# T5-bias attention with a bilinear FFN: a new order for the opening's loads and steps

## The chip, the cores and the metric

The kernel runs on one core of a Trainium2 chip. The metric is the device time of one execution in microseconds; smaller is better. Engines: PE (TensorE, matmuls and transposes), DVE (VectorE), ACT (ScalarE), POOL (GpSimd) and SP (SyncE, which here only issues DMAs).

## The reference

Eight batches of eight heads, 576 positions, head size 64. Each head's scores get a bias that depends on the distance of the two positions alone (32 buckets), then softmax and the product with the values. The result, 4608 tokens of 512 features, goes through a bilinear FFN without a nonlinearity.

```python
scores = scale * np.matmul(q, k.transpose(0, 1, 3, 2))      # q, k, v: 8 x 8 x 576 x 64
bias = bias_table[bucket]                                   # bucket from |i - j|, 32 x 8 table
scores = scores + bias.transpose(2, 0, 1)[None, :, :, :]
attn = softmax(scores)
x = (attn @ v), heads side by side                          # 4608 x 512
a = x @ w_a                                                 # 512 x 1536
b = x @ w_b
out = (a * b) @ w_out                                       # 1536 x 512
```

## The kernel before

**Tiling.** A *pair* is two neighbouring heads of one batch; pairs are numbered 0 to 31, four to a batch. The 576 positions are 512 main ones (four tiles of 128) and a tail of 64. Scores are kept with the keys on the partitions, so exponentials come out of ACT as the left operand of the product with the values, which carries a column of ones for the softmax's sum. The bias is applied after the exponential: it is multiplied by exp(bias), taken from *band* tiles `W` (one for each head pair; `Wt` for the tail) that DVE reads backwards. A band depends on the distance alone: the 32 x 8 table is read, its last row is subtracted, ACT takes the exponential, PE spreads it over 256 distances with a one-hot matrix, DVE copies that into a row of ones, SP stores it to DRAM (`bias_tab`), and DMAs read it back with one step of offset for each partition. A filler is a matmul on a tile of zeros (`warm_up`).

**The opening and the steady part.** Pairs 0 to 7 (batches 0 and 1) and the first FFN layer on batch 0's 512 main tokens are done by an opening that is written out by hand as a list of tokens, `opening`, which `step` turns into instructions one by one. Each engine takes its own instructions in the list's order. Pairs 8 to 31 follow in a steady part (`steady`, `slot_step`) that weaves their attention with the FFN of earlier batches. In the opening q and k are transposed on PE; from batch 2 on by DMA.

**Tokens** (the first digit is the pair p, or the FFN's block of 128 hidden features):

- `<name` issues a load: q, k (`k23` is pairs 2 and 3; `q123h0` is the first 256 positions of q of pairs 1 to 3), v0, v1 (batch 0's values, heads 0 to 3 and 4 to 7), t and u (tails of q and k of batches 0 and 1), vt (tails of v), W and R (upper and lower columns of a band), Wt, wa, wb, wo (FFN weights, in thirds). All go to POOL's queue except `W0`, on SP. They are all issued ahead of the opening's other tokens in program order.
- `YQ0`, `YK0`: pair 0's q and k, loaded as fp32 on SP by `load_first`, are converted to bf16. `TQ`, `TK`, `TZ`: PE transposes of q, k and tails (`TQ00` is the first half of the queries of pair 0; `TQ0` does both); `CQ`, `CK`, `CZ`: their copies out of PSUM.
- `Sphu`: score matmuls of pair p, query half h, key tiles 2u and 2u+1 (pairs 4 to 7: `Spt`, one key tile). `E` their exponential on ACT, `M` the multiplication by the band on DVE. `KS`, `EK`: the tail keys of all four pairs of batch 0. `T`, `ET`, `MT`: a pair's tail.
- `AVph`: product with the values; `N`: normalisation; `X`, `CX`: PE transpose and copy to `xn`, the FFN's input. `V`: copy of the values next to their ones.
- `FA`, `FB`, `HA`, `G`: one block of x @ w_a and x @ w_b on PE, the first's copy on ACT, their product on DVE (a, b: first and second 256 tokens; f: all 512).
- `PV`, `PC`, `PU`, `PX`, `PF`: zeroing of padding. `w2`: two fillers. `LH`, `LV`, `TH`: loads and DMA transposes for batch 2.
- `:A` is ACT, `:D` DVE.

The scores of the first four pairs share two PSUM buffers with tails, so a score half waits until the exponential before the last has read its buffer. What the change touches:

```python
    nc.sync.dma_start(out=cn_sb[:, :], in_=cn_handle.ap())            # one-hot matrix and identity
    load_first(q, kq32[1])                                            # L228
    load_first(k, kq32[0])
    nc.scalar.dma_start(out=bt_sb[0:NB, :], in_=bias_table)           # L234; bl_sb (the last row): L235
    warm_up(5)
    ...
    pad_z(0, 0)                                                       # zeroes half of ZB[0], L193
    pad_z(0, 1)
    nc.vector.tensor_copy(out=tab_sb[0:H, c0:c0 + NR], in_=tps[0:H, 0:NR])   # L260; the store to bias_tab: L268
```

Lines of the profile that the text uses: L129 and L153 loads of q, k, v; L263 bands; L281 FFN weights; L329 DVE copies; L474 scores (`qkh`), L480 their exponential (`ath`); L696 FFN matmuls (`pa`, `pb`).

Of the kernel before, what the change touches and what calls it, by code (L numbers as in the profile page):

```python
# [13 lines left out]
def kernel(  # L14
# [11 lines left out]
    nc = tc.nc  # L26
# [5 lines left out]
    B, H, S, Dh = 8, 8, 576, 64  # L32
    NB = 32
# [27 lines left out]
    NR = 256  # L61
# [127 lines left out]
    def load_w_out():  # L189
        nc.gpsimd.dma_start(out=wo_sb[:, :, :], in_=moe_w_out.rearrange("(t p) n -> p t n", p=128))  # L190

    def pad_z(b, hh):
        nc.vector.memset(ZB[b][64 * hh:64 * hh + 64, :, :, Dh - Dh * hh:128 - Dh * hh], 0.0)  # L193
# [3 lines left out]
        nc.vector.memset(tl[i][64:128, :, :, 0:Dh], 0.0)  # L197

    def pad(eng, x, p0, p1):
        if eng is nc.vector:  # L200
            nc.vector.memset(x, 0.0)
            return
        n = int(np.prod(x.shape[1:]))
        z = (zero_sb.bitcast(FP32) if x.dtype == FP32 else zero_sb)[p0:p1, 0:n]
        if len(x.shape) == 3:
            z = z.rearrange("p (a b) -> p a b", b=x.shape[2])
        elif len(x.shape) == 4:
            z = z.rearrange("p (a b c) -> p a b c", b=x.shape[2], c=x.shape[3])
        nc.scalar.activation(out=x, in_=z, func=ACTF.Copy)
# [17 lines left out]
    def load_first(x, dst):  # L227
        nc.sync.dma_start(out=dst.rearrange("p (h x) -> p h x", x=256),  # L228
                          in_=x[0, 0:2, 0:SM, :].rearrange("h (p t) d -> p h (t d)", t=NM))

    nc.sync.dma_start(out=cn_sb[:, :], in_=cn_handle.ap())
    load_first(q, kq32[1])
    load_first(k, kq32[0])
    nc.scalar.dma_start(out=bt_sb[0:NB, :], in_=bias_table)  # L234
    nc.scalar.dma_start(out=bl_sb[0:NB, :],  # L235
                        in_=bass.AP(tensor=bias_table.tensor, offset=(NB - 1) * H,
                                    ap=[[0, NB], [1, H]]))
    nc.vector.memset(zero_sb[:, :], 0.0)
    nc.vector.memset(tab_sb.bitcast(FP32)[0:H, :], TWO_ONES)
    pad_ones(0)  # L240
# [5 lines left out]
    def warm_up(n, dst=None):  # L246
        for _ in range(n):
            nc.tensor.matmul(out=(warm if dst is None else dst)[:, :], lhsT=zero_sb[:, 0:128],
                             rhs=zero_sb[:, :], start=True, stop=True)

    warm_up(5)
    nc.scalar.activation(out=eb_sb[0:NB, :], in_=bt_sb[0:NB, :], func=ACTF.Exp)
    tps = ps_ff.tile([128, 512], FP32, tag="ffn", name="tab_ps")
    nc.tensor.matmul(out=tps[0:H, 0:NR], lhsT=eb_sb[0:NB, :], rhs=oh_sb[0:NB, :],
                     start=True, stop=True)
    warm_up(2)
    c0 = S - 1 - NR // 2
    pad_z(0, 0)
    pad_z(0, 1)
    nc.vector.tensor_copy(out=tab_sb[0:H, c0:c0 + NR], in_=tps[0:H, 0:NR])  # L260

    def load_w(hp, y0, y1, eng):
# [22 lines left out]
    def load(name):  # L285
        if name[0] in "qk" and name[1:2].isdigit():
            ps, _, half = name[1:].partition("h")
            p0, n = int(ps[0]), len(ps)
            if half:
                load_qh(2 * p0, 2 * p0 + 2 * n, int(half))  # L290
            else:
                b, h = divmod(2 * p0, H)
                (load_q if name[0] == "q" else load_k)(b, h, h + 2 * n)
        elif name[0] in "tu":
            load_compact(int(name[0] == "u"), int(name[1] == "k"))
        elif name in ("v0", "v1"):
            load_v(0, 4 * int(name[1]), 4 * int(name[1]) + 4)
        elif name[:3] == "vb1":
            load_v(1, *((0, 4) if name[3] == "a" else (4, 8)))
        elif name[:2] == "vt":  # L300
            load_vt_part(int(name[2] == "1"), "ab".index(name[-1]))
        elif name == "wo":
            load_w_out()
        elif name[:2] == "Wt":
            load_wt("ab".index(name[2]))
        elif name[0] in "WR":
            load_w(int(name[1]), *((320, NY) if name[0] == "W" else (0, 320)), nc.sync if name in ('W0',) else nc.gpsimd)
        else:
            load_weights(*((moe_w_a, wa_sb) if name[1] == "a" else (moe_w_b, wb_sb)), int(name[2]))

# [478 lines left out]
    def v_next(s):  # L789
# [7 lines left out]
    ACT = nc.scalar  # L797

    opening = """
        <q123h0 <k1 <tk <vtb <k23 <W1 <W0 <v0 <vta <tq <W2 <W3 <v1 <Wta <q123h1 <R0 <Wtb <R1 <k4 <wa0  # L800
        <wb0 <R2 <uq <q5 <q4 <R3 <k5 <wa1 <q7 <wb1 <k6 <uk <k7 <vb1a <vb1b <vt1a <q6 <wb2 <vt1b <wa2 <wo
        PC0:A PX0:D YQ0:A PC1:A PU0:D PV0:A PX1:D TQ0 YK0:D TK0 CQ00:A CQ01:D CK0:D TQ10 PF1:A CQ10:D
        S000 E000 PV1:D S001 E001 TK1 CK1:D TQ30 TZ1 CZ1:D S011 CQ30:D E011 S101 TQ20 CQ20:D E101 M101
        S100 E100 TK3 CK3:D KS EK M000 TK2 S301 E301 CK2:D w2 S200 E200 M100 M001 w1 S201 E201 V0:D
        PU1:D w2 S300 E300 M200 M201 AV00 TZ0 AV10 S010 CZ0:A N00 T0 N10 E010 X10 X00 CX00:A V1:D AV20
        CX10:A TQ11 TQ21 M301 M300 ET0 AV30 CQ11:A S110 CQ21:A N20 M010 M011 PW:A MT0 S111 TQ31 E110 X20
        CQ31:A E111 T1 ET1 N30 M110 X30 CX20:D CX30:D AV01 T2 TK4 M111 S210 ET2 E210 FA0a HA0a N01 T3
        MT1 X01 AV11 CK4:D CX01:A PF0:D LH ET3 N11 S211 E211 FB0a FA1a HA1a X11 G0a MT2 CX11:D S310 E310
        FB1a G1a S311 M210 FA2a FB2a HA2a E311 TQ5 TQ4 CQ4:A M211 FA3a AV21 CQ5:A S42 G2a S43 FB3a TZ0x
        MT3 M311 HA3a M310 TK5 E42 N21 FA4a HA4a CZ0x:D AV31 LV CK5:D X21 E43 TQ7 CQ7:A G3a N31 S41 E41  # L810
        S52 E52 FB4a FA5a HA5a CX21:D G4a M43 TK6 X31 CX31:D FB5a S40 E40 CK6:D S53 G5a FA0b HA0b TZ1x
        M41 CZ1x:D FB0b G0b S51 E53 FA1b HA1b TK7 FB1b FA2b E51 M52 HA2b CK7:D S50 G1b V2:D FB2b FA3b
        E50 V3:D G2b HA3b T4 M40 FB3b G3b S70 M42 ET4 MT4 FA4b FB4b T5 HA4b M53 E70 G4b TQ6 ET5 M51
        CQ6:A AV40 N40 FA5b S71 E71 S73 MT5 M50 FB5b HA5b AV41 S72 E73 G5b N41 M71 FA6f M73 T6 E72 M72
        ET6 MT6 AV50 FB6f HA6f N50 S62 S61 E62 G6f M62 FA7f HA7f AV51 N51 TH S60 E61 M61 FB7f G7f E60
        M60 S63 E63 FA8f HA8f T7 ET7 M63 M70 FB8f G8f AV60 FA9f FB9f N60 MT7 AV70 HA9f G9f FA10f HA10f
        FB10f N70 AV71 G10f FA11f HA11f FB11f N71 X71 AV61 X70 G11f N61 CX71:D CX70:D
    """

    h0 = (0, 1)  # L820
# [2 lines left out]
    def step(token):  # L823
# [6 lines left out]
            load(token[1:])  # L830
            return
        name, _, e = token.partition(":")
        eng = ACT if e == "A" else nc.vector
        kind = name.rstrip("0123456789abfx")
        num = name[len(kind):]
        if kind in ("FA", "HA", "FB", "G"):
# [21 lines left out]
        if kind == "TQ":  # L858
            tr_qh(p, i[1]) if len(i) > 1 else tr_q(p)
        elif kind == "CQ":  # L860
            copy_qh(p, i[1], eng) if len(i) > 1 else copy_q(p, eng)
        elif kind == "TK":
            tr_k(p)
        elif kind == "CK":
            copy_k(p, eng)
        elif kind == "TZ":
            tr_tails(second, p)
        elif kind == "CZ":
            copy_tails(second, p, eng)
        elif kind == "KS":  # L870
            tail_keys0()
        elif kind == "EK":
            ex_keys0()
        elif kind == "S":
            qk_half(p, i[1], (i[2],)) if first else qk(p, 0, (i[1],))
        elif kind == "E":
            ex_half(p, i[1], i[2]) if first else ex(p, i[1])
        elif kind == "M":
            mul_half(p, i[1], i[2]) if first else mul(p, i[1])
        elif kind == "T":  # L880
            qk_tail(p)
        elif kind == "ET":
            ex_tail(p)
        elif kind == "MT":
            mul_tail(p)
        elif kind == "V":
            b, g = divmod(p, 2)
            v_in(b, 4 * g, 4 * g + 4, eng)
        elif kind == "AV":
            av_mm(p, jqs, *((ps_ff, "ffn") if first and i[1] == 0 and p % 2 else ()))  # L890
        elif kind == "N":
            av_norm(p, jqs)
            if 4 <= p < 7 and i[1] == 1:
                t_x(p)
        elif kind == "X":
            tr_x(p, jqs)
        elif kind == "CX":
            copy_x(p, jqs, eng)
        elif kind == "YK":
            copy(eng, kn[0][:, 0:512], kq32[0])  # L900
        elif kind == "YQ":
            copy(eng, qn[0][:, 0:512], kq32[1])
        elif kind == "PV":
            pad_vt(0, p, eng)
        elif kind == "PC":
            pad_vt(1, p, eng)
        elif kind == "PU":
            pad_blocks(ZB[1], p, eng)
        elif kind == "PF":
            pad_blocks(tl[0], p, eng)  # L910
        elif kind == "PX":
            pad_x(p, eng)
        elif kind == "PW":
            copy(eng, Wt_sb[:, :, 0:64], Wt_sb[:, :, 64:128])
        elif kind == "LH":
            load_k(2, 0, 4)
            load_q(2, 0, 4)
            load_tails(2)
            load_v(2, 0, 4)
        elif kind == "TH":  # L920
            t_half(2, 0)
        elif kind == "LV":
            load_vt(2)
        else:
            raise ValueError(token)
# [187 lines left out]
```

## Time and profile before

| | us |
|---|---|
| median of 3 runs | 400.9 (400.34 to 401.28) |
| profiled execution, device time | 401.12 |
| its span in the profile | 399.3 |
| PE busy, idle | 390.6, 8.7 |
| DVE, ACT, POOL busy | 240.9, 255.9, 133.4 |

The span is what the trace covers; 1.8 us of the device time lie around it. A row of the timeline has the start in us, the busy time, the engine, the line, the operation with its output and inputs, the count, and in brackets the idle time of the engine before it and what ended that. Durations overlap when instructions of one engine follow each other, so a step counts by the distance of the starts where the rows show it. Times in the text are us from the span's start.

### The profile page before, as it was taken

Reading aid. Unit: us, or ns where it says so; the run is one execution under the profiler, and the core shown is the slowest. Engines: PE = TensorE matmul, PEld = TensorE weight load, DVE = VectorE, ACT = ScalarE, POOL = GpSimd, SP = SyncE. Lnnn points to the kernel's source line nnn. Section 1 sums busy time; section 2 is a strip of 40 time slices with the busy share of each in tenths; the row PEclk is TensorE's granted clock in tenths of the full one; section 3 lists DMA queues with packets and bytes.
Section 4 is the critical chain, followed back from the end, with each engine's and each line's share of the span. In section 5 each row is a group of like instructions: output and inputs, shape, how many; then the busy total and the mean of one; then the engine's idle time right before and its main releaser. Section 6 shows DMA issues by size and latency. Waiting matters only on the chain.

```text
span 399.3 us, 13162 instructions
## 1 busy us (share of the span) xinstructions
PE 390.6 (98%) x5614; PEld 231.2 (58%) x5626; DVE 240.9 (60%) x565; ACT 255.9 (64%) x386; POOL 133.4 (33%) x199
## 2 busy tenths in 40 slices
PE   6999999999999999999999999999999999999996
PEld 2477655566665666566656665666666654444443
DVE  4799997547754775477756875487547752321420
ACT  4898994568766876587748774777568733323321
POOL 5966531739751885019700880000000000000000
PEclk9999999999999999999999999999999999999999
DMA  8999999899996999729992999161420012002004
GB/s 140 185 204 198 205 158 133 82 188 132 154 152 130 107 168 120 151 57 140 128 123 69 139 122 151 56 99 26 99 80 19 17 29 108 2 26 79 2 0 105
DMA packets 136618, 42.78 MB, mean 107 GB/s; under 512 B 114184, under 2 KB 131816, under 8 KB 136560
## 3 DMA queue, kind: packets, MB, share of 16 engines
q0 software_dynamic: 81120, 19.88, 54.5%
q1 hardware_dynamic: 50096, 12.76, 23.3%
q10 hardware_dynamic: 5344, 9.31, 7.1%
q8 instruction: 44, 0.72, 0.8%
q14 instruction: 14, 0.11, 0.1%
HBM read 39.23 MB, written 9.45 MB: 122 GB/s over the span
## 4 chain that ended last, share of the span: by engine, by line
PE 95%; DMA 1%; ACT 1%; DVE 0%; issue 0%; ACTq 0%; SPq 0%
PE ffn_pair L606 25%; PE ffn L606 24%; PE av L606 8%; PE pb L696 8%; PE pa L696 8%; PE score L606 7%; PE po L733 6%; PE av L589 2%; PE qkh L474 1%; DMA xn<-in_k_dram 1%; PE qk L606 1%; PE qr L444 1%; PE av L583 1%; PE trb L337 1%; PE trk L337 1%; ACT ath L480 0%
## 5 line engine op out<-in xcount | busy, mean ns | idle before, releaser
L458 ACT ACTIVATE at<-score 128x1024 bf16<-128x1024 f32 x96 | 98.4, 1025 | 36.7 <-PE score L606 33.3
L463 DVE TENSOR_TENSOR at<-at,W 128x1024 bf16<-128x1024 bf16 x112 | 74.7, 686 | 26.4 <-ACT at L458 18.1
L606 PE MATMUL ffn_pair<-xn,wb 64*128 64x512 bf16 x288 | 81.8, 376 | 0.0
L606 PE MATMUL ffn_pair<-xn,wa 64*128 64x512 bf16 x288 | 81.8, 376 | 0.0
L606 PE MATMUL ffn<-xn,wa 64*128 64x512 bf16 x288 | 79.9, 377 | 0.0
L606 PE MATMUL ffn<-xn,wb 64*128 64x512 bf16 x288 | 79.6, 375 | 0.0
L606 PE MATMUL av<-vm,at 64*128 64x65 bf16 x1536 | 63.4, 190 | 0.0
L606 PEld LDWEIGHTS <-at 64*128 64x128 bf16 x1536 | 48.8, 94 | 21.8 <-issue 1.2
L606 PEld LDWEIGHTS <-wa 64*128 64x128 bf16 x576 | 47.0, 94 | 17.5
L606 PEld LDWEIGHTS <-wb 64*128 64x128 bf16 x576 | 47.3, 94 | 11.6 <-issue 0.7
L706 DVE TENSOR_TENSOR g<-pb,ha 128x512 bf16<-128x512 f32 (+1 forms) x42 | 25.8, 615 | 44.7 <-PE pb L696 44.2
L606 PEld LDWEIGHTS <-g 64*128 64x128 bf16 x624 | 33.4, 94 | 24.1 <-issue 0.4
L606 PE MATMUL ffn_pair<-wo,g 64*128 64x512 bf16 x336 | 44.0, 376 | 0.0
L703 ACT ACTIVATE ha<-pa 128x512 f32<-128x512 f32 (+1 forms) x42 | 22.6, 538 | 31.9 <-PE pa L696 28.0
L138 POOL DMA_DIRECT2D qn<-in_q_dram x48 | 36.0, 781 | 11.2 <-DMA wo<-in_moe_w_out_dram 7.3
L696 PE MATMUL pb<-xn,wb 128*128 128x512 bf16 (+1 forms) x165 | 37.9, 349 | 0.3
L606 PE MATMUL score<-QB,KB 64*128 64x512 bf16 x192 | 37.9, 376 | 0.0
L696 PE MATMUL pa<-xn,wa 128*128 128x512 bf16 (+1 forms) x163 | 37.5, 348 | 0.2
L147 POOL DMA_DIRECT2D kn<-in_k_dram x48 | 35.8, 759 | 3.4 <-issue 2.2
L606 PE MATMUL av<-vm,att 64*128 64x65 bf16 x384 | 36.6, 190 | 0.0
L706 DVE TENSOR_TENSOR g<-ffn_pair,ha 128x512 bf16<-128x512 f32 x36 | 24.9, 692 | 18.5 <-ACT ha L703 18.0
L606 PE MATMUL ffn<-wo,g 64*128 64x512 bf16 x288 | 35.0, 376 | 0.0
(125 smaller groups left out, 603.1 us busy)
## 6 DMA issues: line engine op xcount, KB each, us to landing
out_dram<-QKT ACTq DMA_DIRECT2D x32, 256.0 KB, 2.0
vn<-in_v_dram POOLq DMA_DIRECT2D x16, 256.0 KB, 5.4
kn<-in_k_dram POOLq DMA_DIRECT2D x48, 64.0 KB, 4.7
qn<-in_q_dram POOLq DMA_DIRECT2D x48, 64.0 KB, 4.2
wa<-in_moe_w_a_dram POOLq DMA_DIRECT2D x3, 512.0 KB, 8.4
wb<-in_moe_w_b_dram POOLq DMA_DIRECT2D x3, 512.0 KB, 8.3
wo<-in_moe_w_out_dram POOLq DMA_DIRECT2D x1, 1536.0 KB, 16.2
xn<-XG SPq DMA_TRANSPOSE x54, 3.9
```

Source lines behind the costliest of these rows:

```text
L138: nc.gpsimd.dma_start(out=by_tile(qn[b % 2])[:, h0 // 4, t, :, :], in_=q[b, h0:h1, 128 * t:128 * t + 128, :].transpose([1, 0, 2]))
L147: nc.gpsimd.dma_start(out=by_tile(kn[b % 2])[:, h0 // 4, t, :, :], in_=k[b, h0:h1, t:SM:NM, :].transpose([1, 0, 2]))
L337: nc.tensor.transpose(ps[64 * hh:64 * hh + 64, 128 * t:128 * t + 128], src[b][:, o:o + 64], ident[:, :])
L444: nc.tensor.matmul(out=rows[hh][:, ST * t:ST * t + ST], lhsT=kT[r, t, :], rhs=z[r, 0, ST * hh:ST * hh + ST], start=True, stop=True)
L458: nc.scalar.activation(out=at[:, :, :], in_=ps[:, :, :], func=ACTF.Exp, scale=scale)
L463: nc.vector.tensor_tensor(out=at[:, :, :], in0=at[:, :, :], in1=w[:, :, S - 1 + t:S - 1 + t - SM:-1], op=MULT)
L589: nc.tensor.matmul(out=pav[:, slot, hh, :], lhsT=weights(p, t, hh, jq), rhs=vm[i][:, 2 * hp + hh, t, :], start=False, stop=True, skip_grou ...
L606: i = nc.tensor.matmul(out=o, lhsT=lhs[r], rhs=rhs[r], start=first, stop=last, skip_group_check=True)
L696: nc.tensor.matmul(out=ps[:, 0:n], lhsT=w[df // 4][:, mc, 128 * (df % 4):128 * (df % 4) + 128], rhs=xn_sb[mc][:, 512 * c + lo:512 * c + lo ...
L703: nc.scalar.activation(out=ha[:, 0:n], in_=ff["pa", df, lo][:, 0:n], func=ACTF.Copy)
L706: nc.vector.tensor_tensor(out=g_sb[df][:, lo:lo + n], in0=ff["pb", df, lo][:, 0:n], in1=ff["ha", df, lo][:, 0:n], op=MULT)
L733: nc.tensor.matmul(out=po[:, :], lhsT=g_sb[df][:, 128 * tt:128 * tt + 128], rhs=wo_sb[:, df, :], start=(df == 0), stop=(df == NDF - 1))
```

## The change

The constant with the one-hot matrix and the identity is no longer read in one piece on SP: the one-hot part goes to ACT's queue, the identity (`<id`) to POOL's as its first load. The bias table's two reads go first on ACT and SP. `YQ0` moves from ACT to DVE, ahead of `YK0`. One of the first five fillers goes. The two zeroings of `ZB[0]` become tokens (`PZ`). `PV0`, `PC0` and `PC1` go to POOL, between its loads. `W1` joins `W0` on SP. The order of the loads and of all other tokens of the opening is new; the steady part stays. The whole diff:

```diff
--- before.py
+++ after.py
@@ -197,8 +197,8 @@
         nc.vector.memset(tl[i][64:128, :, :, 0:Dh], 0.0)
 
     def pad(eng, x, p0, p1):
-        if eng is nc.vector:
-            nc.vector.memset(x, 0.0)
+        if eng is not nc.scalar:
+            eng.memset(x, 0.0)
             return
         n = int(np.prod(x.shape[1:]))
         z = (zero_sb.bitcast(FP32) if x.dtype == FP32 else zero_sb)[p0:p1, 0:n]
@@ -228,13 +228,13 @@
         nc.sync.dma_start(out=dst.rearrange("p (h x) -> p h x", x=256),
                           in_=x[0, 0:2, 0:SM, :].rearrange("h (p t) d -> p h (t d)", t=NM))
 
-    nc.sync.dma_start(out=cn_sb[:, :], in_=cn_handle.ap())
+    nc.scalar.dma_start(out=bt_sb[0:NB, :], in_=bias_table)
+    nc.sync.dma_start(out=bl_sb[0:NB, :],
+                      in_=bass.AP(tensor=bias_table.tensor, offset=(NB - 1) * H,
+                                  ap=[[0, NB], [1, H]]))
+    nc.scalar.dma_start(out=oh_sb[0:NB, :], in_=cn_handle.ap()[0:NB, 0:NR])
     load_first(q, kq32[1])
     load_first(k, kq32[0])
-    nc.scalar.dma_start(out=bt_sb[0:NB, :], in_=bias_table)
-    nc.scalar.dma_start(out=bl_sb[0:NB, :],
-                        in_=bass.AP(tensor=bias_table.tensor, offset=(NB - 1) * H,
-                                    ap=[[0, NB], [1, H]]))
     nc.vector.memset(zero_sb[:, :], 0.0)
     nc.vector.memset(tab_sb.bitcast(FP32)[0:H, :], TWO_ONES)
     pad_ones(0)
@@ -248,15 +248,13 @@
             nc.tensor.matmul(out=(warm if dst is None else dst)[:, :], lhsT=zero_sb[:, 0:128],
                              rhs=zero_sb[:, :], start=True, stop=True)
 
-    warm_up(5)
+    warm_up(4)
     nc.scalar.activation(out=eb_sb[0:NB, :], in_=bt_sb[0:NB, :], func=ACTF.Exp)
     tps = ps_ff.tile([128, 512], FP32, tag="ffn", name="tab_ps")
     nc.tensor.matmul(out=tps[0:H, 0:NR], lhsT=eb_sb[0:NB, :], rhs=oh_sb[0:NB, :],
                      start=True, stop=True)
     warm_up(2)
     c0 = S - 1 - NR // 2
-    pad_z(0, 0)
-    pad_z(0, 1)
     nc.vector.tensor_copy(out=tab_sb[0:H, c0:c0 + NR], in_=tps[0:H, 0:NR])
 
     def load_w(hp, y0, y1, eng):
@@ -301,10 +299,12 @@
             load_vt_part(int(name[2] == "1"), "ab".index(name[-1]))
         elif name == "wo":
             load_w_out()
+        elif name == "id":
+            nc.gpsimd.dma_start(out=ident, in_=cn_handle.ap()[:, NR:])
         elif name[:2] == "Wt":
             load_wt("ab".index(name[2]))
         elif name[0] in "WR":
-            load_w(int(name[1]), *((320, NY) if name[0] == "W" else (0, 320)), nc.sync if name in ('W0',) else nc.gpsimd)
+            load_w(int(name[1]), *((320, NY) if name[0] == "W" else (0, 320)), nc.sync if name in ('W0', 'W1') else nc.gpsimd)
         else:
             load_weights(*((moe_w_a, wa_sb) if name[1] == "a" else (moe_w_b, wb_sb)), int(name[2]))
 
@@ -797,24 +797,26 @@
     ACT = nc.scalar
 
     opening = """
-        <q123h0 <k1 <tk <vtb <k23 <W1 <W0 <v0 <vta <tq <W2 <W3 <v1 <Wta <q123h1 <R0 <Wtb <R1 <k4 <wa0
-        <wb0 <R2 <uq <q5 <q4 <R3 <k5 <wa1 <q7 <wb1 <k6 <uk <k7 <vb1a <vb1b <vt1a <q6 <wb2 <vt1b <wa2 <wo
-        PC0:A PX0:D YQ0:A PC1:A PU0:D PV0:A PX1:D TQ0 YK0:D TK0 CQ00:A CQ01:D CK0:D TQ10 PF1:A CQ10:D
-        S000 E000 PV1:D S001 E001 TK1 CK1:D TQ30 TZ1 CZ1:D S011 CQ30:D E011 S101 TQ20 CQ20:D E101 M101
-        S100 E100 TK3 CK3:D KS EK M000 TK2 S301 E301 CK2:D w2 S200 E200 M100 M001 w1 S201 E201 V0:D
-        PU1:D w2 S300 E300 M200 M201 AV00 TZ0 AV10 S010 CZ0:A N00 T0 N10 E010 X10 X00 CX00:A V1:D AV20
-        CX10:A TQ11 TQ21 M301 M300 ET0 AV30 CQ11:A S110 CQ21:A N20 M010 M011 PW:A MT0 S111 TQ31 E110 X20
-        CQ31:A E111 T1 ET1 N30 M110 X30 CX20:D CX30:D AV01 T2 TK4 M111 S210 ET2 E210 FA0a HA0a N01 T3
-        MT1 X01 AV11 CK4:D CX01:A PF0:D LH ET3 N11 S211 E211 FB0a FA1a HA1a X11 G0a MT2 CX11:D S310 E310
-        FB1a G1a S311 M210 FA2a FB2a HA2a E311 TQ5 TQ4 CQ4:A M211 FA3a AV21 CQ5:A S42 G2a S43 FB3a TZ0x
-        MT3 M311 HA3a M310 TK5 E42 N21 FA4a HA4a CZ0x:D AV31 LV CK5:D X21 E43 TQ7 CQ7:A G3a N31 S41 E41
-        S52 E52 FB4a FA5a HA5a CX21:D G4a M43 TK6 X31 CX31:D FB5a S40 E40 CK6:D S53 G5a FA0b HA0b TZ1x
-        M41 CZ1x:D FB0b G0b S51 E53 FA1b HA1b TK7 FB1b FA2b E51 M52 HA2b CK7:D S50 G1b V2:D FB2b FA3b
-        E50 V3:D G2b HA3b T4 M40 FB3b G3b S70 M42 ET4 MT4 FA4b FB4b T5 HA4b M53 E70 G4b TQ6 ET5 M51
-        CQ6:A AV40 N40 FA5b S71 E71 S73 MT5 M50 FB5b HA5b AV41 S72 E73 G5b N41 M71 FA6f M73 T6 E72 M72
-        ET6 MT6 AV50 FB6f HA6f N50 S62 S61 E62 G6f M62 FA7f HA7f AV51 N51 TH S60 E61 M61 FB7f G7f E60
-        M60 S63 E63 FA8f HA8f T7 ET7 M63 M70 FB8f G8f AV60 FA9f FB9f N60 MT7 AV70 HA9f G9f FA10f HA10f
-        FB10f N70 AV71 G10f FA11f HA11f FB11f N71 X71 AV61 X70 G11f N61 CX71:D CX70:D
+        <id <q123h0 <k1 <tk <vtb <k23 <v0 PV0:P <vta <tq <v1 PC0:P PC1:P <W2 <W3 <W1 <W0 <q123h1
+        <vt1a <R0 <uk <Wta <vt1b <k4 <q4 <Wtb <uq <k6 <R1 <R2 <wa0 <wb0 <k5 <R3 <q6 <q5 <wa1 <wb1
+        <q7 <k7 <vb1a <vb1b <wb2 <wa2 <wo
+        YQ0:D YK0:D w2 TQ0 CQ01:D CQ00:D TK0 TQ20 CK0:D PZ0 PZ1 TQ10 CQ20:A PU0:D PX0:D S000 PV1:D
+        TK1 CQ10:A E000 CK1:D S001 TZ1 CZ1:D S101 E001 TK2 S100 CK2:D TK3 E101 S201 E100 E201 PX1:D
+        CK3:D TQ30 V0:D CQ30:D S010 E010 PU1:D TZ0 S200 S300 w1 CZ0:D V1:D M100 E200 E300 M101 M201
+        KS M001 S301 M000 TQ21 TQ31 EK T0 CQ31:D E301 CQ21:A w2 S011 M300 ET0 TQ11 LH AV00 M010
+        S211 M200 CQ11:D E011 TQ4 E211 TK4 S210 AV10 N00 S311 M301 CK4:D AV20 E210 CQ4:D N10 PW:A
+        X00 X10 M011 E311 AV30 S111 CX00:A CX10:A S110 TZ1x N20 MT0 N30 X20 E111 CX20:D CZ1x:D M111
+        E110 AV01 T1 X30 T2 CX30:D ET1 N01 FA3a M110 MT1 ET2 FA2a S40 HA2a TZ0x HA3a T3 E40 X01
+        CX01:D FB2a MT2 CZ0x:A AV11 G2a FA0a TK6 ET3 N11 TK5 S43 M210 S310 HA0a FB0a CK6:A E310
+        CK5:D FB3a E43 TQ6 TQ5 M211 CQ5:A AV21 G0a S41 S42 CQ6:A M310 G3a FA1a MT3 E41 HA1a N21 X11
+        FB1a M311 T4 E42 G1a CX11:D FA4a AV31 LV M41 FA5a HA4a S53 ET4 N31 X21 FB4a X31 HA5a FB5a
+        MT4 CX31:D E53 CX21:D S50 S51 TK7 G4a G5a E50 E51 TQ7 FA3b FA7f M42 S52 M40 HA3b S63 V2:D
+        CQ7:D FB7f HA7f M43 AV40 E52 FB3b M50 G7f E63 FA2b CK7:D T5 N40 PF0:D PF1:D AV41 ET5 G3b
+        M51 HA2b V3:D FA8f S60 M53 S62 HA8f FB2b MT5 E60 M52 FB8f E62 T6 N41 G2b M62 AV50 G8f FA1b
+        S71 N50 ET6 S61 FA5b HA1b E71 MT6 FB1b AV51 HA5b G1b M63 E61 FB5b FA4b S73 G5b N51 TH HA4b
+        M60 S72 E73 FB4b G4b E72 M61 FA6f S70 FB6f M73 HA6f FA9f E70 T7 HA9f G6f M71 FA10f ET7 M72
+        HA10f AV60 FB9f M70 MT7 FA11f N60 AV71 G9f FB10f HA11f FA0b N71 AV70 G10f HA0b FB11f N70
+        X71 FB0b G11f G0b AV61 CX71:A N61 X70 CX70:A
     """
 
     h0 = (0, 1)
@@ -830,7 +832,7 @@
             load(token[1:])
             return
         name, _, e = token.partition(":")
-        eng = ACT if e == "A" else nc.vector
+        eng = {"A": ACT, "P": nc.gpsimd}.get(e, nc.vector)
         kind = name.rstrip("0123456789abfx")
         num = name[len(kind):]
         if kind in ("FA", "HA", "FB", "G"):
@@ -906,6 +908,8 @@
             pad_vt(1, p, eng)
         elif kind == "PU":
             pad_blocks(ZB[1], p, eng)
+        elif kind == "PZ":
+            pad_z(0, p)
         elif kind == "PF":
             pad_blocks(tl[0], p, eng)
         elif kind == "PX":
```

## The prediction

> **What bounds the kernel now.** I read the page's head and its slices first, then the busy time by stretch.
>
> ```profile
> PE 390.6 (98%) x5614; PEld 231.2 (58%) x5626; DVE 240.9 (60%) x565; ACT 255.9 (64%) x386; POOL 133.4 (33%) x199
> ```
>
> By stretch (busy time of each engine with its instructions, then granted clock, DMA share, GB/s):
>
> ```profile
> 0.00:30.00 30.00, 25.65 (x336) 15.18 (x338) 21.61 (x64) 23.53 (x37) 21.52 (x34) 1.00 1.13 177
> 30.00:60.00 30.00, 29.84 (x364) 19.22 (x364) 27.95 (x78) 27.45 (x42) 16.51 (x24) 1.00 1.48 186
> ...
> 390.00:399.30 9.30, 5.53 (x50) 3.69 (x48) 0.29 (x1) 1.85 (x4) 0.00 (x0) 1.00 0.44 103
> ```
>
> PE is idle for 8.7 us of 399.3: 4.35 in the first 30, 3.8 at the end, next to nothing between. So the time is PE's work plus what PE loses before it is saturated, and only the opening can give or take. The change keeps PE's work except for one filler of 12, in the first 4 us, where nothing useful waits behind it. The question is therefore: at the first FFN matmul (FA0a before, FA3a after), from which PE always has something to do, how late is it, and how much other PE work is already done? Next I read the timeline of that stretch.
>
> ```profile
> 1.24 0.78 POOL L153 DMA_DIRECT2D qn<-in_q_dram  x1 [0.80 <-POOLq L1097]
> ...
> 6.64 0.43 DVE L329 CAST kn<-xn 128x512 bf16<-128x512 f32 x1 [1.58 <-DMA xn<-in_k_dram]
> ...
> 8.31 1.04 PE L474 MATMUL qkh<-QKT 64*128 64x256 bf16 x8 [0.20 <-DVE QKT L329]
> ...
> 8.52 0.72 POOL L263 DMA_DIRECT2D W<-bias_tab  x1 [3.71 <-DMA bias_tab<-wo]
> ...
> 11.06 2.85 ACT L480 ACTIVATE ath<-qkh 128x1024 bf16<-128x1024 f32 x3 [0.17 <-PE qkh L474]
> ...
> 16.29 0.61 PE L474 MATMUL qkh<-QKT 64*128 64x256 bf16 x4
> ...
> 17.25 0.39 PE L474 MATMUL qkh<-QKT 64*128 64x256 bf16 x4
> ...
> 17.54 0.86 POOL L281 DMA_DIRECT2D wa<-in_moe_w_a_dram  x1
> ...
> 27.45 0.61 PE L696 MATMUL pa<-xn,wa 128*128 128x256 bf16 x4
> ```
>
> The first score half (S000) starts at 8.31, held by k's landing at 6.62. POOL's load queue stands still from 4.8 to 8.5 behind W1, which waits for the table. Exponentials follow each other at 0.92 to 0.97 us (three in 2.85). Four score matmuls take 0.61 at 16.29 and 0.39 at 17.25: PE doubles its speed near 17.0. Saturation is reached about 25, and FA0a starts at 27.45.
>
> **The start.** On SP q and k keep their places (issued 1.18 and 1.72), but behind 1 KB of bias row instead of the 96 KB constant. POOL gets the identity as its first load, so q123h0 is issued at 1.95 instead of 1.24. K's landing: no row says how much the 96 KB cost. Upper bound 6.6, since nothing is added on its queue; lower 5.45 (96 KB at the 206 GB/s of 4 to 5 us is 0.47, and POOL's competing load starts 0.7 later). I take 6.1. Behind it on VectorE now stand CQ01 and CQ00, waiting with q long done: 0.43 for YK0, three copies at 0.34 to 0.42, so CK0 ends 1.5 to 1.7 after the landing (1.64 before) and S000 could start at 7.75. But TQ20 and TQ10 (before, TQ10 alone) now precede S000 on PE and need q123h0: 1.95 plus the 5.2 of its row is 7.15, plus two times 0.35 to 0.42 (before full speed), gives 7.95. The later decides: **S000 at 7.95, 0.35 earlier** (bounds 7.5 and 8.4). YQ0 on VectorE (0.43 against ACT's 0.63) and the two extra fillers before TQ0 lie before k's landing and cost nothing; if k came at 5.45 the fillers (end near 5.3) would still be covered.
>
> **The table.** With both bias loads first in their queues the second lands about 0.45 earlier; ACT's table load, ending at 2.93, then holds the exponential to 2.95 instead of 3.27. The store goes at 4.05 instead of 4.38. W1 and W0 follow on SP at about 7.9 and 8.3 and land, by the 2.6 and 3.3 of their rows, by 11.6. Their first reader M100 stands on VectorE behind CK3, V0, CQ30, PU1, CZ0 and V1, beyond 14: worth nothing. The zeroing PZ0, PZ1 (0.64 together) moves from before the table copy to after CK0, into VectorE's wait for TK1 (1.0 idle there before).
>
> **8 to 17 us.** PE's list now has nine score halves by KS and S301 (nine times 0.54 is 4.9), TK1 to TK3 (1.7), TZ1, TZ0, TQ30 (0.8), one filler (0.43), KS (0.97): 8.8, plus about 0.35 of waiting for a score buffer that an exponential holds, from 7.95 to 17.1. Before, seven score halves were done by 17.0, with 1.05 us of fillers and a gap of 0.34. The new list turns the earlier start and the fillers into two score halves and TZ0.
>
> **17 us to the first FFN matmul.** At the full-speed rows: TQ21 and TQ31 0.42, three T 1.65, fillers 0.43, six S 2.0, TQ11 0.21, AV00 to AV30 2.85, TQ4 and TK4 0.68, four X 0.54, TZ1x 0.22, AV01 0.9: 9.9. Waits: T0 on EK, S011 on E301, T2 on E110, about 0.25 each. **FA3a at 27.75**, 0.3 later than FA0a. ACT agrees: from E000 at 8.6, sixteen exponentials at 0.92 to 1.02 and 2.2 of other work end E110 at 25.5 to 27.1. VectorE too: from CK3 near 12.1 it has 15 us of copies, multiplies and normalisations up to CX30, 27.2. Bounds 27.0 (no waits) and 28.3 (durations 1.02 and no overlap).
>
> **What is done by then.** Against before: S211 and S311 (0.66), TQ4 (0.34), TZ1x (0.22): 1.22 us of PE work that before lay behind FA0a. Net: 0.3 minus 1.22, **a gain of 0.92**.
>
> **The loads.** The value loads, the new order and the identity move wa0 from 19th to 26th of POOL's queue. Twenty-five issues at 0.70 from 1.24, plus three zeroings on POOL, give its issue. No row has that zeroing; the nearest are 0.10 (POOL's 128x1 constant), 0.28 (VectorE, same tile), 0.40 (ACT). I take 0.3 each, nearest to the same tile, with 0.1 to 0.5 as bounds. So wa0 goes at 19.65 instead of 17.54, the 3.7 us hole paying for most of the way.
>
> The DMA view, two of its issues (engine, count, size, us from issue to landing):
>
> ```profile
> wa<-in_moe_w_a_dram POOLq DMA_DIRECT2D x1, 512.0 KB, 7.3
> ...
> wb<-in_moe_w_b_dram POOLq DMA_DIRECT2D x1, 512.0 KB, 9.1
> ```
>
> By these rows wa0 lands at 26.95 (needed 27.75) and wb0, issued 0.75 later, at 29.5. FB2a stands behind FA3a, FA2a, S40, TZ0x, T3 and X01 (2.4 us), at 30.2. Both are covered by some 0.7. If that cover is gone, every us of lateness is a us of time, because PE takes its list in order.
>
> On a port shared by two engines: VectorE's copy of the values (V0) took 0.72 beside a POOL issue at 16.44 and V1 took 0.42 at 20.74, while POOL's issues stayed at 0.62 to 0.86 beside VectorE work. The Trainium skill, "SBUF — State Buffer", section "SBUF: two separate sides", says that a VectorE copy in its two-port mode locks GpSimd out of writing descriptors until it ends; by that rule the sum would be the one of the held port, below. The rows show at most a tenth or two on POOL's side, so the sum stays as it is.
>
> **After 28 us.** VectorE has about 39 us of work in the 43 until the steady part (before about 41), ACT about 33; before it was tighter and PE lost 0.16 in 30 to 60. I add nothing, with 0.5 as upper bound.
>
> **Rivals.**
> Even (0.09): q123h0 lands at 7.9 or k at 6.6, S000 gains nothing, and FB2a waits 0.3 for wb0. For it: two more things stand before S000. Against it: 96 KB less ahead of k. Gain 0.92 − 0.35 − 0.3, about 0.3: 400.6.
> Late weights, slower (0.17): the place is FA3a, PE's in-order list behind it, the price one for one. POOL's queue must move 4.3 MB up to and including wa0, SP's and ACT's loads counted. At the 206 GB/s that most single microseconds from 16 to 24 show, from 2.7 on, it is through at 23.6, below the sum's own 26.95; at the 159 GB/s that the rows of 10 to 17 us average, it ends at 29.7, FA3a is 2.0 later than forecast, and the time is 402.0. It decides from a landing of 28.7 on (401 even), 29.5 for slower by 0.2%. Against it: those rows were thin because POOL issued small loads, not because the engines were full.
> Held port (0.03): YQ0, YK0, V0 and V1 (0.43, 0.43, 0.72, 0.42) each stop a POOL queue that before stood idle beside YK0; wa0 is issued 1.9 later, lands at 28.85, and FA3a is 1.1 later: 401.1. Against it: POOL's durations above.
> Late clock (0.08): the doubling near 17.0 depends on what PE did before. If it came one step of about 3.4 us later, half of that is lost, 1.7, of which PE's waits absorb up to 0.65: 401.1 to 401.7. For it: more transposes and fewer full-height fillers before 15. Against it: KS, w1 and S301 fill 15.1 to 17.1 nearly without a gap. The Trainium skill, "TensorE: Matmul & The Clock Gate", Part 1, says that PE runs at half rate until one free-running window of some 3.4 us has been busy; that PE was dense here from 8.3 and doubled only at 17.0 agrees with a busy share being needed, and no row shows the window itself.
> That the change doesn't do what it says I exclude: every token names its engine and order.
>
> **The numbers.** The profiled execution took 401.12 with a span of 399.3; minus 0.92 that is 400.2 with a span of 398.4, and from the median, 0.2 lower, 400.0. The three runs lie 0.94 apart, so about 0.2%, 0.8 us, is what a measurement can tell. The forecast case has 0.63, with its own range 398.8 (FA3a at 27.0) to 400.7 (FA3a at 28.3 or 0.5 of stalls): 0.52 of it beyond 0.8, 0.11 within. Same: 0.11, the even case 0.09, half of the late clock 0.04, the held port 0.03. Slower: late weights 0.17, the other half 0.04. The range, 398.6 to 402.1, leaves out the far end of late weights and a start better than all bounds.
>
> **What would show it.** S000 near 7.95 and E000 near 8.6; no 3.7 us hole in POOL; nine first halves done at 17.1 with the doubling near 17; wa0 issued at 19.65 and landed before 28; FA3a at 27.75; the chain on PE without a gap of over 0.2 after it; the first steady score pair at 69.9 instead of 70.84. I am wrong if FA3a waits for a load, if PE's matmuls are still slow at 18, or if PE is idle more than 0.5 us between 28 and 70.

## The result and the profile after

The changed kernel takes 402.48 us (median of 20 runs, 400.52 to 405.12). The kernel before, on the same chip and in the same comparison, takes 401.27 (median of 20, of which one took 574.88 and is left out of the ratio; the other 19 have the same median). The ratio is 1.0028, with a 95% interval of 1.0015 to 1.0041: slower by 0.28%, some 1.2 us, a little over what a measurement can tell. I had forecast 400.0, and 402.1 as the far end.

The profiled execution took 402.05 us with a span of 400.3; before it was 401.12 and 399.3. (Lines 261, 274 and 279 of the rows below, bands, tails of v and FFN weights, are lines 263, 276 and 281 of before.) The page's head, and the busy time by stretch (length, then busy time and count of PE, PEld, DVE, ACT, POOL, then granted clock, DMA share, GB/s):

```profile
PE 389.2 (97%) x5612; PEld 231.5 (58%) x5625; DVE 241.6 (60%) x568; ACT 252.9 (63%) x380; POOL 133.9 (33%) x202
```

```profile
0.00:30.00 30.00, 23.78 (x313) 14.48 (x315) 20.93 (x62) 19.98 (x26) 24.96 (x41) 0.83 1.15 169
30.00:60.00 30.00, 29.47 (x379) 20.31 (x380) 28.84 (x85) 26.59 (x43) 11.98 (x17) 1.00 1.38 189
...
14.00:18.00 4.00, 2.00 (x14) 0.82 (x16) 3.13 (x6) 3.82 (x5) 2.34 (x4) 0.57 1.39 194
18.00:24.00 6.00, 6.00 (x76) 3.89 (x78) 4.22 (x10) 3.44 (x5) 5.91 (x10) 0.50 1.10 158
```

PE is idle 6.22 us of the first 30 (4.35 before), and the granted clock of that stretch has fallen from 1.00 to 0.83. From 18 to 24 PE has work without a gap, at a clock of 0.50: 76 matmuls, where the kernel before did 127 in the same stretch.

The timeline of the opening, in the rows that answer to those of before:

```profile
5.32 0.43 DVE L329 CAST kn<-xn 128x512 bf16<-128x512 f32 x1 [0.27 <-DMA xn<-in_k_dram]
...
7.95 0.39 PE L474 MATMUL qkh<-QKT 64*128 64x256 bf16 x4
...
8.59 7.45 ACT L480 ACTIVATE ath<-qkh 128x1024 bf16<-128x1024 f32 x8
...
12.33 0.73 POOL L261 DMA_DIRECT2D W<-bias_tab  x1 [0.45 <-DMA vn<-in_v_dram]
...
15.38 0.62 POOL L274 DMA_DIRECT2D vt<-in_v_dram  x1 [0.98 <-DVE vm L329]
...
16.12 0.61 PE L474 MATMUL qkh<-QKT 64*128 64x256 bf16 x4
...
16.63 0.71 POOL L129 DMA_DIRECT2D kn<-in_k_dram  x1 [0.63 <-DMA W<-bias_tab]
...
17.95 0.64 PE L346 MATMUL trb<-cn_sb,qn 64*64 64x64 bf16 x16 [1.22 <-DMA qn<-in_q_dram]
...
21.62 0.83 POOL L279 DMA_DIRECT2D wa<-in_moe_w_a_dram  x1
...
25.28 0.39 PE L474 MATMUL qkh<-QKT 64*128 64x256 bf16 x4
...
29.95 1.04 PE L696 MATMUL pa<-xn,wa 128*128 128x256 bf16 x8
```

Four score matmuls take 0.39 us already at 7.95, 0.61 at 16.12, and 0.39 again at 25.28. By these rows and the granted clock in short windows PE was at full speed from 7.7, lost it at 14.5 and had it back at 24.8; before, it switched once, at 17.1. (The expectations below say 7.2, 14.7 and 24.4, a first reading of the rows.) POOL's 3.7 us hole is gone, but three waits for landings have come, 2.06 us in all, and `wa0` is issued at 21.62. In the DMA view:

```profile
qn<-in_q_dram POOLq DMA_DIRECT2D x1, 192.0 KB, 7.4
...
wa<-in_moe_w_a_dram POOLq DMA_DIRECT2D x1, 512.0 KB, 7.3
```

So `wa0` lands at 28.92 and `wb0` at 31.5. This time FA3a did not wait for it, since PE itself came only at 29.95. A second profiled execution of the same kernel (401.78 us, span 400.0) had PE at half speed until 19.5 and at full speed from there, and there the loads were what ended the wait:

```profile
29.62 1.05 PE L696 MATMUL pa<-xn,wa 128*128 128x256 bf16 x8 [1.01 <-DMA wa<-in_moe_w_a_dram]
...
32.17 0.61 PE L696 MATMUL pb<-xn,wb 128*128 128x256 bf16 x4 [0.41 <-DMA wb<-in_moe_w_b_dram]
```

A third (401.79 us) had full speed from 12.3 to 15.7, half until 22.5, and FA3a at 29.15 without a wait for `wa0`, which had landed at 28.34. Three executions, three histories of PE's speed, and FA3a at 29.15 to 29.95 in all, 1.4 to 2.2 later than forecast.

### The profile page after: what moved, and what is told of

Read it like the earlier page. It is cut to its first block, busy times and chain, and to the rows that moved or that the text cites. A ratio compares the mean times of both kernels' runs of the same rounds, so it can differ in the third digit from the quotient of the medians.

```text
span 400.3 us, 13162 instructions
## 1 busy us (share of the span) xinstructions
PE 389.2 (97%) x5612; PEld 231.5 (58%) x5625; DVE 241.6 (60%) x568; ACT 252.9 (63%) x380; POOL 133.9 (33%) x202
## 4 chain that ended last, share of the span: by engine, by line
PE 86%; DVE 5%; POOL 2%; DMA 2%; ACT 2%; issue 1%; ACTq 1%; DVEq 0%; POOLq 0%
PE ffn_pair L606 24%; PE ffn L606 24%; PE av L606 8%; PE pb L696 7%; PE score L606 7%; PE pa L696 7%; PE po L733 6%; DMA qn<-in_q_dram 2%; PE av L589 1%; DVE ath L489 1%; DVE XG L645 1%; DVE g L706 1%; PE qr L444 1%; DVE at L463 1%; ACT at L458 0%
## 5 line engine op out<-in xcount | busy, mean ns | idle before, releaser
L606 PEld LDWEIGHTS <-g 64*128 64x128 bf16 x624 | 33.6, 94 | 24.0 <-issue 0.4
L703 ACT ACTIVATE ha<-pa 128x512 f32<-128x512 f32 (+1 forms) x42 | 22.5, 539 | 30.6 <-PE pa L696 26.7
```

Source lines behind the costliest of these rows:

```text
L606: i = nc.tensor.matmul(out=o, lhsT=lhs[r], rhs=rhs[r], start=first, stop=last, skip_group_check=True)
L703: nc.scalar.activation(out=ha[:, 0:n], in_=ff["pa", df, lo][:, 0:n], func=ACTF.Copy)
```

## The experiments

My theory after the first profile was that PE's speed, lost at 14.5 after a thin stretch, costs the time; the rival was the late weights, which cap FA3a near 29 whatever PE does. The ratios below are to the kernel before on the same chip, with 95% intervals; its median there lay at 401.06 to 401.35.

**Fillers and the load that PE waited for (x1, x2, x3).** x1 adds six fillers to PE's list, x2 moves `<q123h1` (it ended PE's 1.22 us wait) up four places (two in POOL's own queue, since `W1` and `W0` go on SP), x3 does both:

```diff
-TK3 E101 S201 ... CQ30:D S010 E010 PU1:D TZ0 S200 S300 w1
+TK3 E101 w1 S201 ... CQ30:D w1 S010 E010 PU1:D TZ0 w2 S200 w2 S300 w1
-PC0:P PC1:P <W2 <W3 <W1 <W0 <q123h1
+PC0:P PC1:P <q123h1 <W2 <W3 <W1 <W0
```

> The changed kernel with six more fillers in PE's list between 11 and 15 us (one before S201, one before S010, two before S200, two before S300), where PE waits for the exponentials. Clock theory (PE got full speed at 7.2 us, lost it at 14.7 because it was idle for half of 13 to 15, and ran at half speed until 24.4): the granted clock stays 1.00 through 14 to 24, FA3a starts near 28.3 instead of 29.95, the time falls by 1 to 1.6 us to about 401 (ratio to before 0.999 to 1.001). Late-load theory (PE waits 1.2 us for q123h1, landed at 17.95): the wait at 17 remains, the time stays near 402.4 (ratio 1.003).

> The changed kernel with one load moved: q123h1 ahead of the bands W2 and W3 on POOL's queue, two places earlier. Late-load theory: it lands about 1.5 us earlier, near 16.4, PE's wait of 1.2 us at 17 is gone, the time falls by about 1 us to 401.4 (ratio to before 1.000). Clock theory: the wait goes, but PE is still at half speed from about 15 to 24 and what it gains there it spends waiting for the exponentials' buffers; the time falls by 0.3 at most (ratio 1.002 to 1.003).

> Both edits: the six fillers and q123h1 two places earlier. Both causes at work: clock 1.00 throughout, no wait at 17, FA3a near 27.8 as forecast, time 1.5 to 2.2 us below the changed kernel, 400.3 to 400.9 (ratio to before 0.996 to 0.999). Clock theory alone: as with the fillers alone. Late-load theory alone: as with the moved load alone.

Measured: x1 401.86, 1.0017 (1.0001 to 1.0032); x2 403.18, 1.0039 (1.0021 to 1.0057); x3 402.40, 1.0035 (1.0016 to 1.0055). None reaches the kernel before, and no interval lies apart from that of the change as it is. The timelines of x1 and x3 say why (one row of each):

```profile
28.90 1.05 PE L696 MATMUL pa<-xn,wa 128*128 128x256 bf16 x8 [0.47 <-DMA wa<-in_moe_w_a_dram]
```

```profile
29.32 1.05 PE L696 MATMUL pa<-xn,wa 128*128 128x256 bf16 x8 [1.38 <-DMA wa<-in_moe_w_a_dram]
```

PE was ready at 28.43 and 27.94, the latter within 0.2 of the 27.75 that I had worked out, and then stood waiting for `wa0`. In these two executions PE kept its speed once it had it (from 16.7 in x1, 12.2 in x3), and the weights are what is late next.

**The new loads with the old steps (x4).** The list of before, with the new loads (`W1` on SP, the bias reads first, the constant in two parts):

```diff
-<q123h0 <k1 <tk <vtb <k23 <W1 <W0 <v0 <vta ... <wa0 <wb0 ...
+<id <q123h0 <k1 <tk <vtb <k23 <v0 <vta <tq <v1 <W2 <W3 <W1 <W0 <q123h1 <vt1a <R0 ... <wa0 <wb0 ...
 PC0:A PX0:D YQ0:A PC1:A PU0:D PV0:A ...
```

> The changed kernel's loads with the steps of before: bias reads first, identity as POOL's first load, the new order of loads, W1 on SP; every compute token, filler and zeroing as before. Late-load theory: q123h1 and the FFN weights land as in the changed kernel, but the old steps need q123h1 only at 22; wa0 at 29 against FA0a at 27.45 costs 1 to 1.6 us, time about 402.5 (ratio 1.003 to 1.004). Clock theory: the loads are harmless as long as PE's steps are the old ones, full speed comes near 17 and stays, ratio 0.999 to 1.001, unless FA0a waits for wa0.

Measured: 404.91, 1.0089 (1.0063 to 1.0115). The profile is that of its slowest run, 407.36. `wa0` landed at 30.92, and the waits of the trace have

```profile
PE pa L698 <- DMA wa<-in_moe_w_a_dram: 2.4, 1, 2.4
```

The loads alone make the kernel before 3.6 us slower; the new steps take some of it back.

**The weights late in the kernel before (y4).** One line of its loads:

```diff
-<k4 <wa0 <wb0 <R2 <uq <q5 <q4 <R3 <k5 <wa1
+<k4 <R2 <uq <q5 <q4 <R3 <k5 <wa0 <wb0 <wa1
```

> The kernel before with wa0 and wb0 six places later in POOL's queue, behind R2, uq, q5, q4, R3 and k5, nothing else changed. Late-weights theory: wa0 is issued near 21.9 instead of 17.54, lands near 29, FA0a waits for it and starts 1.5 us later, the time rises by 1.2 to 2.0 us (ratio 1.003 to 1.005). Clock-alone theory: the fillers and the steps are those of before, no change (0.999 to 1.001).

Measured: 406.56, 1.0127 (1.0102 to 1.0152), far more than expected. The timeline of the first two groups, and the stretch around the wait:

```profile
30.08 1.01 PE L696 MATMUL pa<-xn,wa 128*128 128x256 bf16 x4 [2.91 <-DMA wa<-in_moe_w_a_dram]
...
34.00 0.61 PE L696 MATMUL pb<-xn,wb 128*128 128x256 bf16 x4
```

```profile
28.00:32.00 4.00, 1.92 (x14) 1.63 (x15) 0.09 (x1) 0.76 (x2) 1.32 (x2) 0.77 1.24 205
```

PE waits 2.91 and comes out of the wait at half speed (until 33.6): FA0a is 2.6 later than before, FB0a 4.2 later (34.00 against 29.77), the kernel 5.3 (406.56 − 401.27). Here a late weight costs more than its lateness, because PE lost its speed in the wait; the prediction's one for one does not hold for it.

**The weights early in the changed kernel (y1, z6).** y1 keeps the steps and moves loads that are needed late behind the weights; z6 adds two moves for the waits that y1's trace showed, 0.7 for `uk` and 0.4 for `k23` (`<uk` ahead of `<wa0`, `<k23` ahead of `<vtb`):

```diff
-<q123h1 <vt1a <R0 <uk <Wta <vt1b <k4 <q4 <Wtb <uq <k6 <R1 <R2 <wa0 <wb0 <k5 <R3 <q6 <q5
+<q123h1 <R0 <Wta <k4 <q4 <Wtb <uq <wa0 <wb0 <uk <R1 <R2 <k6 <k5 <R3 <vt1a <vt1b <q6 <q5
```

> The changed kernel with its loads reordered: wa0 and wb0 go from 26th and 27th to 20th and 21st of POOL's queue, ahead of uk, R1, R2, k6, vt1a and vt1b, none of which is needed before 28 us. Late-weights theory (where PE runs at full speed in time, FA3a is ready at 27.9 to 28.4 but wa0 lands at 28.9 to 29.3, and FB2a waits again 0.35 for wb0): wa0 is issued near 17.5 and lands near 26, no FFN matmul waits for a load, the time falls by 1.0 to 1.7 us against the changed kernel, to 400.8 to 401.4 (ratio to before 0.998 to 1.000). Clock-alone theory (only the moment of PE's full speed costs): no change, ratio 1.003.

> The changed kernel with the load order of the best version (wa0 and wb0 at places 21 and 22, uk ahead of them, k23 one place earlier) and the changed kernel's own fillers. If the loads are the whole loss: the time is that of the best version, 399.8 to 400.5, ratio 0.996 to 0.998. If PE's speed is a loss of its own: no FFN matmul waits for a load, but PE is at half speed in some stretch between 14 and 24, FA3a is later than 28.3, and the ratio stays at 0.999 to 1.002.

Measured: y1 401.42, 1.0013 (0.9995 to 1.0032); z6 400.53, 0.9996 (0.9974 to 1.0017). In z6 `wa0` was issued at 17.15 and landed at 22.55, and no FFN matmul waited for a load. Its timeline and its slow stretch:

```profile
27.87 1.05 PE L696 MATMUL pa<-xn,wa 128*128 128x256 bf16 x8
```

```profile
14.00:18.00 4.00, 3.14 (x33) 1.80 (x34) 3.52 (x8) 3.82 (x5) 3.42 (x6) 0.55 1.36 209
18.00:24.00 6.00, 6.00 (x95) 3.79 (x94) 4.80 (x12) 4.61 (x8) 5.49 (x8) 0.73 1.20 169
```

PE lost its speed here too (the 0.55), yet FA3a came at 27.87: half speed lasted 6.8 us, against 10.2 in the change's first profile, and PE's wait for `q123h1` was 0.25, against 1.22, so the order of the loads acts through that load as well. The profile is that of z6's fastest run, 399.77. By the medians the order of the loads by itself takes away what the change had lost, and leaves a kernel that can't be told from before; but the interval of z6 still touches that of the change (1.0015 to 1.0041), and y1 lies between the two. z6's runs fall into two groups: eight of 399.77 to 401.32, four of 402.25 to 402.89.

**Weights and fillers (y2, z1).** y2 is y1 with x1's fillers and six opening fillers for four; z1 is y2 with z6's two moves and `w2` ahead of S101 and of TK2:

> The same load order, with the six fillers between 11 and 15 us and two more fillers before the table's matmul. Both theories together: full speed comes early in most executions and is not lost, wa0 is there, FA3a starts at 27.8 to 28.2 and the time is 400.0 to 400.9 (ratio 0.996 to 0.999), spread smaller than the changed kernel's. Late weights alone: as with the load order alone. Clock alone: as the changed kernel with the six fillers, 1.002.

> The reordered loads with all fillers so far, and: two fillers more before S101 and two before TK2, where PE stood idle for 0.7 and 0.4 us at full speed and fell to half speed near 11; uk back ahead of wa0 (PE had waited 0.7 us for it), k23 one place earlier. If what is left of the changed kernel's loss is PE's speed and late loads, full speed holds from 8 on in most executions, FA3a starts near 27.6 and the time is 399.8 to 400.6 (ratio to before 0.995 to 0.998). If the new order of steps itself is worth nothing, the ratio stays at 0.999 to 1.001.

Measured: y2 400.84, 0.9999 (0.9984 to 1.0014); z1 400.00, 0.9964 (0.9948 to 0.9979), its ten runs from 399.31 to 401.08. z1 beats both kernels. Its profile was taken on its slowest run (401.08): a wait of 1.3 for `q123h1` at 17 us cost the speed, and FA3a came at 29.54. So z1's usual execution is not the one that its profile shows.

**Zeroings off POOL (y3).** `PV0`, `PC0` and `PC1` go back to ACT, to bring POOL's loads forward:

```diff
-<v0 PV0:P <vta <tq <v1 PC0:P PC1:P
+<v0 PV0:A <vta <tq <v1 PC0:A PC1:A
```

> The changed kernel with the three zeroings PV0, PC0 and PC1 back on ACT. If POOL's time of issue decides when wa0 lands, its issue comes 1.1 us earlier (20.5 instead of 21.6), it lands near 27.9, and the time falls by up to 1.0 (ratio 1.000 to 1.001). If the limit of eight loads in flight decides (POOL waits 0.45, 0.98 and 0.63 for landings between 12 and 17), the waits grow by what the zeroings took, wa0 is issued within 0.3 of 21.6 and the time stays (ratio 1.003).

Measured: 402.94, 1.0053 (1.0033 to 1.0074), and `wa0` at 21.79, no earlier than 21.62. POOL's timeline shows where the 1.1 us went:

```profile
9.63 1.43 POOL L261 DMA_DIRECT2D W<-bias_tab  x2 [1.17 <-DMA bias_tab<-wo]
...
21.79 0.82 POOL L279 DMA_DIRECT2D wa<-in_moe_w_a_dram  x1
```

POOL reached `W2` earlier and waited 1.17 for the table, then 1.8 in three waits for landings. What POOL does between its loads is not what holds `wa0`. Why the time is worse still than the change's I have not settled; the profiled execution had half speed from 11 to 25.

**Fillers in the kernel before (z2, z5).** Is the new order of steps worth anything? I gave the kernel before its own fillers, eight in each:

```diff
-TQ0 YK0:D TK0 ... CZ1:D S011 ... E011 S101 ... M101 S100 ... TK2 S301 ... w2 S200
+TQ0 YK0:D w3 TK0 ... CZ1:D w1 S011 ... E011 w1 S101 ... M101 w1 S100 ... TK2 w1 S301 ... w2 w1 S200
```

z5 has `w1` ahead of TQ0 instead of the one ahead of S200.

> The kernel before with eight more fillers: three after TQ0, where PE waits 1.2 us for k, and one each before S011, S101, S100, S301 and S200. Clock theory: PE reaches full speed before 9 us in most executions instead of at 17, but before's opening is paced by the exponentials up to 25, so the gain is small: ratio 0.997 to 1.000. If the speed before 17 us decides by itself, the gain is that of the doubled rate on 8 us of PE work, over 1.5 us: ratio below 0.996.

> The kernel before with eight more fillers, placed earlier than in the last try: one before TQ0, three after it, one each before S011, S101, S100 and S301. In the last try the executions fell into two groups, 399 to 400.7 and 402.8 to 404.7. If full speed by 9 us makes the first group, more of the executions fall into it and the median is below 401.3. If the new steps are worth the forecast 0.9 us, its fastest executions stay above the best version's 399.3; if they are at 399 or below, the steps are worth nothing.

Measured: z2 403.25, 1.0023 (0.9994 to 1.0051); z5 402.39, 1.0027 (1.0005 to 1.0048). Both scatter: z2 has 398.95, 399.13 and 400.68, and nine runs of 402.76 to 404.69. The profile of z2 is that of its 398.95:

```profile
24.98 0.61 PE L696 MATMUL pa<-xn,wa 128*128 128x256 bf16 x4
```

PE was at full speed from 4.8 on without a break, and FA0a came 2.5 earlier than before. Why the other runs take longer is not shown, since z5's profile too is of one of its shorter times (400.55, full speed from 8.2). By estimate, eight fillers at the 0.43 that one takes at half speed are 3.4 us of PE, which would be lost where the speed comes late.

**Two more profiles of the change (z3, z4).** They are the second and third execution told above.

> The changed kernel once more, one look, to see at which moment PE gets full speed. If that moment differs from execution to execution (7.2 us, lost at 14.7, back at 24.4 in the first profile), this one shows another, and a switch by 13 that lasts lets FA3a be ready near 28 and wait for wa0 until about 29; a switch after 20 delays FA3a to 29.5 or later by PE's own work. If the moment is fixed by the program, the profile repeats the first.

> A third look at the changed kernel, for the same question: another moment of full speed if it differs from execution to execution, the same if not.

## Why the prediction was wrong, step by step

Two steps failed: the sum of POOL's queue, which had no waits, and the one doubling of PE's speed near 17. FA3a starts at the later of two moments, PE being ready and `wa0` having landed. In the three profiled executions PE was ready at 29.95, 28.61 and 29.15, and `wa0` landed at 28.92, 29.62 and 28.34; the forecast had 27.75 and 26.95. Each of the two alone would have made FA3a late.

**The start: the time right, by luck.** S000 came at 7.95 and E000 at 8.59, as worked out, but by another path. `q123h0` had landed at 7.0 and k before 5.32 (`YK0`'s start), below my lower bound of 5.45. What held PE was the table matmul's wait of 0.8 for the one-hot part: it pushed the four fillers behind it, two of them said to cost nothing, and with them TQ0 to 6.01; TQ20 then waited 0.42 for VectorE's copies and started at 7.50. In the two other executions S000 came at 8.15.

**The table: off by 0.7, without effect on the bands.** The store was issued at 4.74, not 4.05, because the one-hot part now arrives last on ACT's queue (the 0.8 above). Nothing waited for `W0` and `W1`.

**8 to 17 us: the assumption of one doubling at 17.0 failed.** I took the moment at which PE doubles as a property of the kernel. In the three profiled executions it fell at 7.7, 19.5 and 12.3. In the first, the full-speed score halves ran into the exponentials, which follow each other at 0.93 (eight in 7.45), so PE waited for score buffers and was busy only 2.2 of the last 3.4 us before 14.5; there it lost the speed, and the 1.22 wait for `q123h1`, which the sum did not have, came on top. The Trainium skill, "TensorE: Matmul & The Clock Gate", Part 1, says that PE is at half rate until a free-running window of some 3.4 us was busy, and that the moment varies from run to run. The three traces agree on the variation, and their stretches between two changes of speed lasted 6.8 and 10.2 us in the first and 3.4 and 6.8 in the third, once, twice or three times that window. The page's table of the states puts the return to half rate after an idle window; at 14.5 PE had been idle for only about a third of such a window. Further down, that Part tells of a kernel that loses the rate through frequent short idle times between groups of matmuls, which is nearer to this trace. The page calls the penalty of the start under 1% of a typical span and advises against fitting to a count of slow matmuls; here the 20 runs of one kernel reach from 400.52 to 405.12, 1.1%, against an effect of 0.3%, though not all of that need be PE's speed.

**17 us to FA3a: the sum was right, but it was not the last.** PE was ready at 27.94 in x3 and FA3a ran at 27.87 in z6, against 27.75, though with other fillers and another history of speed than the sum assumed. In the changed kernel itself it ran at 29.15 to 29.95.

**The loads: the other step that failed.** `wa0` was to go at 19.65 and land at 26.95; in the first profile it went at 21.62 and landed at 28.92. Its 7.3 us were right. Wrong was the sum of POOL's queue, twenty-five issues at 0.70 without a wait: three waits of 0.45, 0.98 and 0.63 make the 2.0 us. (The zeroings took 0.38 each, for 0.3.) In these waits a POOL load goes out only when the load eight places ahead of it has landed (`R0`, POOL's 15th, behind `v0`, the 7th; `vt1b`, the 18th, behind `v1`, the 10th; `k4`, the 19th, behind `W2`, the 11th; `vt1b`'s row names VectorE's copy of v1, which had waited for the same landing), and the loads issued from 9 to 12 us landed after about 7 us (`q123h1` 7.4, `W2` 7.2, `vt1a` 7.0). The profile of before had already shown such a wait, at `wa1`, the 27th, behind `wa0`, the 19th:

```profile
25.11 0.78 POOL L281 DMA_DIRECT2D wa<-in_moe_w_a_dram  x1 [1.68 <-DMA wa<-in_moe_w_a_dram]
```

My reason against the late weights was that the DMA rows of 10 to 17 us were thin because POOL issued small loads; it did not hold in the changed kernel, where POOL stood waiting for landings in that very stretch while 208 GB/s were moved. The rival had the outcome right: its 159 GB/s gave a landing of 29.7 and 402.0; measured are 28.34 to 29.62, 169 GB/s over the first 30 us, and 402.48. But it had FA3a wait for the load, which only one of the three profiles shows. I gave it 0.17. Of the held port there was no sign: `k23` and `v0` were issued beside `YQ0` and `YK0` in 0.81 and 0.80, against 0.79 and 0.77 before.

**What is done by then: right.** The 1.22 us of earlier work is list arithmetic. FA3a at 29.95 is 2.5 later than FA0a was; less 1.22 that leaves 1.28. The first steady score pair, forecast at 69.9, starts 0.49 later than the 70.84 of before:

```profile
71.33 0.39 PE L606 MATMUL score<-QB,KB 64*128 64x512 bf16 x2
```

The first single-head score pair after 110 us starts at 110.77 instead of 109.97, 0.80 later, and the span is 1.0 longer. PE lost 0.53 instead of 0.16 between 30 and 60; the added 0.37 is inside the bound of 0.5. What is regained before 71 us and lost again after it I have not followed. All three signs of being wrong showed: FA3a waited for a load (in the second profile), PE was slow at 18, and it was idle for 0.73 us between 28 and 70.

**The two losses together.** The order of the loads kept FA3a from starting before 28.3 in all three profiled executions, and moving the loads alone is worth 402.48 − 400.53, about 2 us (over two comparisons whose medians of before differ by 0.2); by the two ratios, 1.0028 and 0.9996, it is 1.3. Within one kernel the executions still differ: z6's two groups lie 2 us apart. PE's speed is the likely reason, but that is not shown: only its 399.77 was profiled, and the mean granted clock of its twelve runs (0.987 to 1.000 in the group of eight, 0.987 to 0.996 in the group of four) does not separate them. With loads and fillers both changed (z1) the time is 400.00, the number forecast. That agreement is no proof of the forecast's mechanism: z1 has fillers that the sum did not, and the kernel before with fillers (z2, z5) reaches 398.95 to 399.17 in its best executions, no worse than z1's 399.31. Whether the new order of the steps is worth anything in itself stays open.

## What to carry to other kernels

An in-order load queue is to be summed with its waits: count how many loads may be in flight, and let load n wait for the landing of load n − 8 (or whatever number the trace shows), with the landing times of the stretch that it will then be in. Before ordering loads, write down when each is first read; what is needed last goes behind what opens the long stretch. A step that rests on the moment at which PE changes speed needs several profiles of the same kernel, because one profile shows one of its histories.

## What the runs showed of the hardware

- The moment at which PE reaches full speed is not the kernel's own: 7.7, 12.3 and 19.5 us in three executions of one kernel. It is lost in stretches where PE still works: at 14.5 after 2.2 busy of 3.4 us, and then half speed lasted 10.2 us, more than six of them without a gap in PE's work. The granted clock changed at distances of 3.4 us or twice or three times that (7.7, 14.5 and 24.8 in the first execution, 12.3, 15.7 and 22.5 in the third).
- The granted clock in the profile shows the lost speed (0.50 at 18 to 24 us of the first execution) but not the slow beginning: the kernel before has 1.00 there while its four score matmuls take 0.61. The score rows show both.
- POOL's zeroing of a 64x260 bf16 tile took 0.38, near ACT's 0.40 and above VectorE's 0.28.
